# A gated linear attention followed by a maxout FFN, one core: a reversed scan makes the keys, weights are rounded and first loaded by halves, and the first packing goes out on two queues

## The chip, the cores and the metric

The kernel runs on one core of a Trainium2 chip. The metric is the device time of one execution in microseconds (us); lower is better. The engines are TensorE (PE in the profile; PEld is its weight load), VectorE (DVE), ScalarE (ACT), GpSimd (POOL) and SyncE (SP), which here only issues DMAs. ScalarE issues some too. Each engine works through its own instructions in order.

## The reference

Four batches of eight heads, 768 tokens, 48 features a head. Every head carries a 48x48 state that is decayed by a gate per feature and read by the query. The result, heads side by side, goes through an FFN that takes the maximum of three products.

```python
f = 1.0 / (1.0 + np.exp(-f_logit))
for t in range(S):
    state = f[:, :, t, :, None] * state + np.einsum('bhd,bhe->bhde', k[:, :, t], v[:, :, t])
    y[:, :, t] = np.einsum('bhd,bhde->bhe', q[:, :, t], state)
x = y.transpose(0, 2, 1, 3).reshape(B * S, H * D)           # 3072 x 384
h = np.maximum(np.maximum(x @ w1, x @ w2), x @ w3)          # 384 -> 768
out = h @ w_out                                             # 768 -> 384
```

q, k, v and f_logit come as float32, the four weight matrices as float64.

## The kernel before

**Units.** The tokens are cut into chunks of C = 64. A unit `u` is one chunk of two batches (128 tokens, all eight heads); there are NU = 24, and units 0, 2, 4, ... belong to one pair of batches, 1, 3, 5, ... to the other. Four units make a group (512 tokens), for which one FFN runs: six groups, six FFNs.

**One unit.** Gates, keys and queries are turned so that features lie on partitions: by TensorE through PSUM (`transposed`, with a ScalarE copy out) for units below 8, by VectorE's 32x32 transpose (`turned`) from unit 8 on. `sigmoids` makes the gates. `products` scans the gates forward on VectorE (L264), so that `prod` at token t is the product of the gates of its chunk up to t, held above 2^-80; a zero gate in front of each head's 64 columns together with a 1 in `floor` restarts the scan there. The query becomes `qh` = q * prod (GpSimd, L277). `quotients` takes the reciprocal of `prod` (VectorE, L283, one call per batch of the unit) and GpSimd makes `kh` = k / prod (L284). `keys` transposes `kh` back on TensorE (L297) for the state update and copies it out as `ks` (ScalarE, L299). `pairs` multiplies `kh` with `qh` (L310) and masks the scores (VectorE, L313). `values` multiplies scores with v (L327) and `ks` with v (L336) into one PSUM tile `y`; VectorE adds the old state and multiplies by the chunk's whole product (L343, L344). `finish` adds the old state's part to `y` (L357) and ScalarE evicts it into `xT`, the FFN's input, with the first three head pairs directly (L366) and the last pair through a tile `last` (L363). Six small DMAs, three per half of the partitions, pack `last` into the 16 rows that each 48 leave free in 64 (L371).

**Weights.** The float64 weights are loaded raw, as pairs of 32-bit words (L196), into four `raw` buffers, and rounded to float32 on the chip: `round_begin` makes upper bits (VectorE, L209), the rest from the low word (ScalarE, L212), adds them (GpSimd, L213) and squares the value's high word to find those too small to keep (ScalarE, L215); `round_end` merges in sign and exponent (VectorE, L223) and writes the weight or zero (VectorE, L226). A buffer is loaded anew after its `round_end`. There are 15 pieces: six of 128 columns of the three input matrices, six of 256 columns, three of 256 rows of `w_out`.

**The FFN.** `ffn` is a generator. It has 18 steps (six column blocks j, three matrices i): three kt matmuls each, 512 tokens wide (L382; the trace counts each as two), then a ScalarE copy for i = 0 (L386) or a VectorE maximum (L388). Behind them come four output steps with `w_out` (L399). In the first FFN each of the steps also rounds pieces that are needed later.

**The order** is written out by hand: units 0 to 3 first, without any FFN; then, from unit 4 on, each unit's parts with `fill(n)` between them, which takes n steps of the FFN of the group before. PSUM holds two `p` tiles for the FFN, two `tr` tiles for transposes and one tile each for scores and `y`. DMAs are issued in the order of the code on the queue named: nearly all on SyncE; before, the packing of units 0 to 2 goes to ScalarE's queue, that of unit 3 half to each. All DMAs share eight semaphores in turn, so each issue waits until the DMA that last used its semaphore has landed, on whichever queue that one was.

A second program, `general`, would run if a chunk's whole product (`ends`) fell below 2^-64; it does not with these inputs.

## Time and profile before

| | us |
|---|---|
| median of 3 runs | 551.06 (550.12 to 552.51) |
| the profiled execution | 553.05 |
| its span, first to last instruction | 551.3 |
| busy: TensorE, its weight loads | 475.6, 256.5 |
| busy: VectorE, ScalarE, GpSimd | 263.7, 127.2, 102.2 |
| first FFN matmul | 72.07 |
| first matmul of the second FFN | 187.26 |

A row of the profile's timeline gives start, duration, engine, line of the kernel, operation, tile written <- tiles read, their shape and, in brackets, how long the engine had idled before and what released it. SPq and ACTq are the DMA issues of SyncE and ScalarE. A row of groups gives the count, busy time in all, the mean of one in ns, and the idle time before them with its releasers. A row of waits gives the total, the number of times and the longest. The granted TensorE clock was 0.924 of full on average.

### The profile page before, as it was taken

The numbers are of one execution on the slowest core, as the hardware profiler recorded it, in microseconds if no ns is written. First come the engines' busy times: TensorE is split into PE (matmuls) and PEld (weight loads), VectorE is DVE, ScalarE is ACT, GpSimd is POOL, SyncE is SP. The second block draws the span as 40 slices with busy tenths as digits, with TensorE's granted clock in tenths as the row PEclk, the third lists the DMA queues.
The fourth block names the chain that finished last, engine by engine and source line by source line (L and its number), as shares of the span: only waits on it lengthen the run. The fifth ranks groups of instructions, "written<-read, shape, count | busy, mean of one in ns | idle before, by whom it ended". The sixth has DMA issues, their size and how long they took to land.

```text
span 551.3 us, 10105 instructions
## 1 busy us (share of the span) xinstructions
PE 475.6 (86%) x4067; PEld 256.5 (47%) x4067; DVE 263.7 (48%) x321; ACT 127.2 (23%) x297; POOL 102.2 (19%) x139
## 2 busy tenths in 40 slices
PE   3654067757979999999999999999999999999994
PEld 2544033333635554556445565454564445544452
DVE  5665017849457546562467545555643762011210
ACT  3253033332522122023202221222032111210000
POOL 3440014445242101220122012121201220000000
PEclk9766577959789999999999999999999999999998
DMA  9454979521251450622613515406236000100002
GB/s 135 89 139 89 175 135 168 119 61 59 37 71 44 59 86 13 78 44 50 99 33 45 77 36 74 77 9 87 42 55 97 18 4 5 47 15 0 0 15 50
DMA packets 166761, 34.99 MB, mean 63 GB/s; under 512 B 155952, under 2 KB 163632, under 8 KB 166704
## 3 DMA queue, kind: packets, MB, share of 16 engines
q1 hardware_dynamic: 163920, 33.68, 35.6%
q10 hardware_dynamic: 2784, 0.57, 0.6%
q8 instruction: 34, 0.56, 0.4%
q14 instruction: 23, 0.19, 0.1%
HBM read 28.31 MB, written 4.72 MB: 60 GB/s over the span
## 4 chain that ended last, share of the span: by engine, by line
PE 76%; DVE 6%; SPq 4%; DMA 3%; issue 3%; ACT 2%; POOL 2%; ACTq 2%; DVEq 0%; POOLq 0%
PE p L382 48%; PE p L399 17%; DVE inv L283 2%; PE y L357 2%; SPq L145 2%; PE y L327 2%; PE a L310 2%; PE tr L297 2%; SPq L196 2%; ACTq L371 2%; PE y L336 1%; DMA raw<-in_moe_w_dram 1%; POOL top_bits L213 1%; PE tr L237 1%; DMA xT<-last 1%
## 5 line engine op out<-in xcount | busy, mean ns | idle before, releaser
L382 PE MATMUL p<-xT,w_in 128*128 128x512 f32 x648 | 296.0, 609 | 23.7 <-DMA xT<-last 21.0
L382 PEld LDWEIGHTS p<-xT,w_in 128*128 128x128 f32 x648 | 122.4, 194 | 167.0 <-issue 157.6
L399 PE MATMUL p<-w_out,hm 128*128 128x384 f32 x288 | 95.3, 488 | 0.0
L283 DVE RECIPROCAL inv<-prod 128x256 f32<-128x256 f32 x48 | 82.0, 1730 | 0.3
L399 PEld LDWEIGHTS p<-w_out,hm 128*128 128x128 f32 x288 | 54.2, 190 | 38.0 <-issue 2.4
L388 DVE TENSOR_TENSOR top<-p,top 128x512 f32<-128x512 f32 x36 | 24.8, 688 | 91.1 <-PE p L382 91.1
L386 ACT COPY top<-p 128x512 f32<-128x512 f32 x36 | 21.1, 585 | 191.9 <-PE p L382 191.9
L277 POOL TENSOR_TENSOR qh<-qt,prod 128x512 f32<-128x512 f32 x24 | 28.6, 1193 | 195.2 <-DVE qt L241 176.1
L284 POOL TENSOR_TENSOR kh<-kt,inv 128x256 f32<-128x256 f32 x48 | 36.1, 753 | 77.0 <-DVE inv L283 77.0
L264 DVE TENSOR_TENSOR_SCAN prod<-gate,floor 128x520 f32<-128x520 f32 x24 | 29.7, 1238 | 29.2 <-ACT gate L253 24.0
L388 DVE TENSOR_TENSOR hm<-p,top 128x512 f32<-128x512 f32 x36 | 24.4, 678 | 39.6 <-PE p L382 39.6
L313 DVE TENSOR_TENSOR at<-a,mask 128x512 f32<-128x512 f32 x24 | 16.5, 687 | 52.8 <-PE a L310 52.8
L213 POOL TENSOR_TENSOR top_bits<-top_bits,rest_bits 128x768 uint32<-128x768 uint32 (+1 forms) x15 | 23.8, 1588 | 76.2 <-ACT rest_bits L212 38.5
L402 ACT COPY o<-p 128x384 f32<-128x384 f32 x24 | 11.5, 478 | 112.5 <-PE p L399 94.5
L297 PE MATMUL tr<-ident,kh 128*128 128x128 f32 x88 | 16.4, 318 | 22.3 <-POOL kh L284 22.2
L299 ACT COPY ks<-tr 128x512 f32<-128x512 f32 x22 | 12.9, 585 | 65.7 <-PE tr L297 62.0
L297 PEld LDWEIGHTS tr<-ident,kh 128*128 128x128 f32 x88 | 12.0, 161 | 32.9 <-POOL kh L284 26.4
L327 PEld LDWEIGHTS y<-at,v_ld 64*64 64x64 f32 x768 | 14.7, 145 | 23.2 <-issue 13.1
L327 PE MATMUL y<-at,v_ld 64*64 64x64 f32 x768 | 18.2, 237 | 8.0 <-ACT xT L366 8.0
L366 ACT COPY xT<-y 64x192 f32<-64x192 f32 (+1 forms) x72 | 22.6, 314 | 1.3
L343 DVE TENSOR_TENSOR st<-y,st 128x384 f32<-128x384 f32 x20 | 11.1, 553 | 23.9 <-PE y L336 23.9
L363 ACT COPY last<-y 64x64 f32<-64x64 f32 (+1 forms) x72 | 15.0, 208 | 21.1 <-PE y L357 16.8
(56 smaller groups left out, 278.9 us busy)
## 6 DMA issues: line engine op xcount, KB each, us to landing
v_ld<-in_v_dram SPq DMA_DIRECT2D x48, 96.0 KB, 3.0
out_dram<-o SPq DMA_DIRECT2D x48, 96.0 KB, 2.2
raw<-in_moe_w_dram SPq DMA_DIRECT2D x12, 288.0 KB, 4.3
raw<-in_moe_w_out_dram SPq DMA_DIRECT2D x3, 768.0 KB, 4.3
f_ld<-in_f_logit_dram SPq DMA_DIRECT2D x32, 64.0 KB, 2.5
k_ld<-in_k_dram SPq DMA_DIRECT2D x32, 64.0 KB, 2.5
q_ld<-in_q_dram SPq DMA_DIRECT2D x32, 64.0 KB, 2.5
xT<-last SPq DMA_DIRECT2D x123, 8.0 KB, 1.8
```

The lines of the kernel that those rows point to most:

```text
L213: nc.gpsimd.tensor_tensor(top, top, rest, op=ALU.add)
L264: nc.vector.tensor_tensor_scan(scan.rearrange("p x t -> p (x t)"), gate.rearrange("p x t -> p (x t)"), floor.rearrange("p x t -> p (x t)") ...
L277: nc.gpsimd.tensor_tensor(qh, qt, prod, op=ALU.mult)
L283: nc.vector.reciprocal(d["inv"][:, a], d["prod"][:, a])
L284: nc.gpsimd.tensor_tensor(d["kh"][:, :, a, :], d["kt"][:, a], d["inv"][:, a], op=ALU.mult)
L297: nc.tensor.transpose(tr_s[:, hp, :], kh[:, hp].rearrange("p a t -> p (a t)"), ident)
L327: nc.tensor.matmul(y[o:o + DP, a, hp * C:(hp + 1) * C], lhsT=v_ld[s, 2 * hp + par, :], rhs=d["at"][s, par, hp, :], start=(hp == 0), stop=F ...
L366: nc.scalar.copy(xT[o, :, t0 + a * C:t0 + (a + 1) * C], y[i, a, 0:NK * C].rearrange("p (h t) -> p h t", h=NK))
L382: nc.tensor.matmul(p, lhsT=w_in[i][:, kt, j * 128:(j + 1) * 128], rhs=xT[:, kt, :], start=(kt == 0), stop=(kt == NK - 1))
L386: nc.scalar.copy(top, p)
L388: nc.vector.tensor_tensor(hm[:, j, :] if i == 2 else top, p, top, op=ALU.max)
L399: nc.tensor.matmul(p[:, 0:DM], lhsT=hm[:, j, i * UT:(i + 1) * UT], rhs=w_out[:, j, :], start=(j == 0), stop=(j == NJ - 1))
```

## The change

**Keys and queries.** `products` and `quotients` become `after` and `before`. `after` scans the gates backwards on VectorE (both inputs and the output read with a step of -1), which gives for each token the product of the gates from it to the chunk's end; shifted by one column that is the factor of the keys, and its first column is the chunk's whole product. GpSimd makes `kh` in one call. `before` scans forward as the old kernel did, but starts each head at the reciprocal of the whole product (a reciprocal of 8 columns instead of 2 x 256), so that query times key is what it was. The state is now multiplied by the whole product ahead of its use, by GpSimd, and VectorE only adds.

```diff
-                nc.vector.tensor_tensor_scan(scan.rearrange("p x t -> p (x t)"), gate.rearrange("p x t -> p (x t)"),
-                                             floor.rearrange("p x t -> p (x t)"), 1.0, op0=ALU.mult, op1=ALU.max)
-                nc.gpsimd.tensor_tensor(qh, qt, prod, op=ALU.mult)
-                nc.vector.reciprocal(d["inv"][:, a], d["prod"][:, a])
-                nc.gpsimd.tensor_tensor(d["kh"][:, :, a, :], d["kt"][:, a], d["inv"][:, a], op=ALU.mult)
+            def after(u):
...
+                nc.vector.tensor_tensor_scan(r[:, 0:LEN][:, ::-1], flat(gate)[:, ::-1], flat(from_one)[:, ::-1], 1.0,
+                                             op0=ALU.mult, op1=ALU.max)
+                whole = r[:, 0:LEN].rearrange("p (x t) -> p x t", t=C + 1)[:, :, 1]
+                nc.vector.reciprocal(from_inv[u % 2][:, :, 0], whole)
+                kt = features("k", u)
...
+                nc.gpsimd.tensor_tensor(kh.rearrange("p h a t -> p a h t"), by_batch(kt),
+                                        by_batch(r[:, 1:LEN + 1].rearrange("p (x t) -> p x t", t=C + 1)[:, :, 1:]),
+                                        op=ALU.mult)
+            def before(u):
...
+                nc.vector.tensor_tensor_scan(flat(prod), flat(gate_tiles[u % 2]), flat(from_inv[u % 2]), 1.0,
+                                             op0=ALU.mult, op1=ALU.max)
+                qt = features("q", u)
...
+                nc.gpsimd.tensor_tensor(qh, qt, prod[:, :, 1:], op=ALU.mult)
+                d["qh"] = by_batch(qh)
+                if u >= 2:
+                    d["state"] = work.tile([128, 2 * HP, D], FP32, name="state")
+                    nc.gpsimd.tensor_tensor(d["state"], states[u % 2],
+                                            ends[:, u, :].unsqueeze(2).to_broadcast([128, 2 * HP, D]), op=ALU.mult)
```

In the loop over units, `after(n)` stands where `products(n)` stood, and `before(n)` behind `values(n-1)`, where the first of the two `quotients` stood. On VectorE, the rows from unit 5's first scan to its last operation before the pairs were these (`r_104` and `prod` are scans, `inv` reciprocals, `hm` and `top` FFN maxima, `st` states, the rest rounding):

```order
L264 SCALAR_TENSOR_TENSOR prod<-gate_96,floor 128x520
L388 TENSOR_TENSOR hm<-p,top 128x512
L223 SCALAR_TENSOR_TENSOR top_bits<-raw,top_bits 128x768
L226 SCALAR_TENSOR_TENSOR w_in_65<-size,top_bits 128x3x256
L209 TENSOR_SCALAR top_bits<-raw 128x768
L343 TENSOR_TENSOR st_1_129<-y,st_0_128 128x384
L344 TENSOR_TENSOR st_1_129<-st_1_129,prod 128x384
L283 RECIPROCAL inv<-prod 128x256
L223 SCALAR_TENSOR_TENSOR top_bits<-raw,top_bits 128x768
L226 SCALAR_TENSOR_TENSOR w_in_63<-size,top_bits 128x3x256
L209 TENSOR_SCALAR top_bits<-raw 128x768
L283 RECIPROCAL inv<-prod 128x256
```

and are now

```order
L301 SCALAR_TENSOR_TENSOR r_104<-gate_100,from_one 128x520
L304 RECIPROCAL from_inv_97<-r_104 128x8
L424 TENSOR_TENSOR hm<-p,top 128x512
L245 SCALAR_TENSOR_TENSOR top_bits<-raw,top_bits 128x384
L248 SCALAR_TENSOR_TENSOR w_in_65<-size,top_bits 128x3x128
L233 TENSOR_SCALAR top_bits<-raw 128x384
L376 TENSOR_TENSOR st_136<-y,state 128x384
L316 SCALAR_TENSOR_TENSOR prod<-gate_100,from_inv_97 128x520
```

What `kh` needs moved from the last row to the first; what `qh` needs moved from the first row to the last.

**Weights.** There are 12 pieces now, all of 256 columns (or rows of `w_out`), in five buffers, and each is rounded in two halves of 384 columns: 24 roundings, one in each of the first FFN's steps 0 to 11 and two in each from 12 on. Of the first three pieces the first halves are loaded ahead of the start and the second halves after unit 1.

```diff
+            RAW = 5
...
+                if len(halves) == 1:
+                    c = slice(halves[0] * 128 * words, (halves[0] + 1) * 128 * words)
+                    dst, src = dst[:, :, c], src[:, c]
...
+                if h == 1 and n + RAW < len(pieces):
+                    raw.pop(n, None)
+                    load_weight(n + RAW)
+            rounds = [(3 * (j // 2) + i, j % 2) for j in range(NJ) for i in range(3)]
+            rounds += [(9 + j // 2, j % 2) for j in range(NJ)]
...
+                            for r in [3 + step] if step < 12 else [2 * step - 9, 2 * step - 8][:24 - 2 * step + 9]:
+                                if r < len(rounds):
+                                    round_end(*rounds[r])
+                                if r + 1 < len(rounds):
+                                    round_begin(*rounds[r + 1])
```

**Packing and the order of the start.** `finish` no longer issues the packing DMAs; `pack` does, from SyncE and ScalarE for units 0 to 3, from SyncE later. Units 0 and 1 are packed behind unit 1, units 2 and 3 behind unit 3, and most loads of units 4 to 7 and of further weights come behind that.

```diff
+                for u in range(GRP):
+                    keys(u)
+                    if u == 3:
+                        finish(2, xT)
+                    pairs(u)
+                    if u < 2:
+                        sigmoids(u + 2)
+                        after(u + 2)
+                    values(u)
+                    if u < 2:
+                        before(u + 2)
+                        finish(u, xT)
+                    if u == 1:
+                        for r in rounds[0:3]:
+                            round_begin(*r)
+                        pack(0, xT, both)
+                        pack(1, xT, both)
+                        for n in range(3):
+                            load_weight(n, (1,))
+                        load(GRP)
+                    if u == 3:
+                        for r in rounds[0:3]:
+                            round_end(*r)
+                        round_begin(*rounds[3])
...
+                finish(3, xT)
+                pack(2, xT, both)
+                pack(3, xT, both)
+                load_weight(3)
+                load_weight(4)
+                load_v(GRP)
```

On SyncE, ahead of the first FFN, the packing of unit 3 (`xT<-last`) stood behind weights (`raw`) and the loads of units 4 to 6, of which the last is seen here:

```order
L196 DMA raw<-in_moe_w_dram 48x3x512
L196 DMA raw<-in_moe_w_dram 16x3x512
L145 DMA f_ld_103<-in_f_logit_dram 64x8x48 x2
L145 DMA k_ld_105<-in_k_dram 64x8x48 x2
L145 DMA q_ld_107<-in_q_dram 64x8x48 x2
L145 DMA v_ld_122<-in_v_dram 64x8x48 x2
L371 DMA xT<-last 16x128 x3
```

Now only the second weight halves and unit 4's rows stand ahead of it, and the larger pieces behind:

```order
L217 DMA raw<-in_moe_w_dram 16x3x256
L158 DMA f_ld_110<-in_f_logit_dram 64x8x48 x2
L158 DMA k_ld_112<-in_k_dram 64x8x48 x2
L158 DMA q_ld_114<-in_q_dram 64x8x48 x2
L407 DMA xT<-last 16x128 x6
L217 DMA raw<-in_moe_w_dram 48x3x512
L217 DMA raw<-in_moe_w_dram 16x3x512
```

The packing (three rows of unit 2, three of unit 3) moved ahead of the loads. At the other end of the first FFN the last pieces of `w_out` stood between the packing of units 4 and 5, ahead of the block loads of units 8 and 9 (`32x16x32` and `32x16x16`, 24 DMAs in all):

```order
L196 DMA raw<-in_moe_w_out_dram 128x2x768 x2
L371 DMA xT<-last 16x128 x6
L196 DMA raw<-in_moe_w_out_dram 128x2x768
L371 DMA xT<-last 16x128 x6
L158 DMA f_ld_102<-in_f_logit_dram 32x16x32
L158 DMA f_ld_102<-in_f_logit_dram 32x16x16
```

Now the last one stands behind the 24, whose last two are the first rows here:

```order
L171 DMA q_ld_114<-in_q_dram 32x16x32
L171 DMA q_ld_114<-in_q_dram 32x16x16
L158 DMA v_ld_128<-in_v_dram 64x8x48 x2
L217 DMA raw<-in_moe_w_out_dram 128x2x768
L407 DMA xT<-last 16x128 x6
```

It moved past the block loads, since two rounding steps per FFN step free the buffers in a different order.

214 lines of the change are left out of this document (101 added, 113 removed).

## The prediction

> **What bounds the kernel now.** I read the profile in this order: the busy slices, then two stretches side by side, then the waits, then the timeline of the front. The slices (40 equal parts of the span; tenths busy, and tenths of the TensorE clock granted) show where time can be lost at all.
>
> ```profile
> PE   3654067757979999999999999999999999999994
> PEclk9766577959789999999999999999999999999998
> ```
>
> From slice 13 (about 165 us) on, TensorE is full at full clock; only the first 165 us have holes. Next, busy time by stretch (from:to, length, then TensorE, its weight loads, VectorE, ScalarE, GpSimd; clock, DMA share, GB/s): the first FFN with units 4 to 7 between its steps, and the next group of four.
>
> ```profile
> 72.07:187.26 115.19, 94.11 (x833) 52.14 (x833) 70.02 (x79) 38.55 (x75) 42.79 (x45) 0.85 0.42 83
> 187.26:261.92 74.66, 73.98 (x686) 38.97 (x685) 40.95 (x48) 16.44 (x42) 11.39 (x16) 1.00 0.37 57
> ```
>
> A settled group takes 74.66 us, and TensorE works through 73.98 of it. VectorE has 34 us free there, so nothing saved on VectorE shortens a settled group by more than 0.7 us. What lies behind 187.26 is 551.3 - 187.3 = 364.0 us, and I keep it. The first group took 40.5 us longer than a settled one, and before it lie 72 us of start. The waits (the third from a query of 72 to 187 us on the first group) say why.
>
> ```profile
> PE p L382 <- DMA xT<-last: 21.0, 1, 21.0
> SPq L145 <- DMA xT<-last: 10.3, 4, 3.9
> PE tr L297 <- POOL kh L284: 19.9, 4, 8.9
> ```
>
> TensorE stood 21.0 us for one packing DMA, SyncE's loads waited 10.3 us for packing DMAs, and four times TensorE waited for scaled keys `kh`, which GpSimd makes from VectorE's reciprocals: 19.9 of the 21.1 us that it idled in the first group (115.19 - 94.11). The timeline shows the places in the start:
>
> ```profile
> 18.39 9.16 SPq L145 DMA_DIRECT2D v_ld<-in_v_dram  x4
> ...
> 23.17 0.65 ACT L363 COPY last<-y 128x64 f32<-128x64 f32 x3 [3.34 <-DVE st L346]
> ...
> 24.50 3.96 ACTq L371 DMA_DIRECT2D xT<-last  x6
> ...
> 39.00 0.98 ACT L366 COPY xT<-y 128x192 f32<-128x192 f32 x3
> ...
> 51.92 0.98 ACT L366 COPY xT<-y 128x192 f32<-128x192 f32 x3
> ...
> 68.93 1.87 SPq L371 DMA_DIRECT2D xT<-last  x3
> ```
>
> Unit 3 was evicted (0.65 + 0.98 us of copies) by 52.90, yet half of its packing was issued at 68.93, since on SyncE it stands behind three units' loads and twelve weight DMAs. The FFN began at 72.07.
>
> **The change, part by part. (1) The start, to the first FFN matmul.** At 0.61 an issue (the row of six further down), the four v loads take 2.4 us instead of 9.16 and end at about 21; the twelve half pieces follow by about 27 and land by 30. On ScalarE, unit 0's copies waited 3.34 us for a state behind unit 2's reciprocals (1.73 each, below); these go and a second scan of 1.24 comes, so the copies end at 23.3 by my estimate (24.80 before). `ks` of unit 1 follows at once, not behind six packing issues (3.96 us). From there to unit 1's eviction lie four copies of about 0.6, the eviction of 1.6 and two groups of matmuls: some 6 us, so 29.3 instead of 39.98. Now come three halves to round and the packing of units 0 and 1, moved to here; a half costs ScalarE two copies like the first row; the others are DMAs, with their median time to landing last:
>
> ```profile
> L212 ACT ACTIVATE rest_bits<-raw 128x384 uint32<-128x384 uint32 x6 | 3.3, 555 | 7.1 <-issue 3.9 <-DMA raw<-in_moe_w_dram 3.1
> xT<-last ACTq DMA_DIRECT2D x21, 8.0 KB, 2.5
> raw<-in_moe_w_out_dram SPq DMA_DIRECT2D x3, 768.0 KB, 4.3
> ```
>
> 3 x 2 x 0.555 = 3.3 and six issues 4.0 bring `ks` of unit 2 to 36.6. From it the path runs through that copy (0.6), six groups of small matmuls at half clock (1.1 each, the next fence), a state add (0.6) and two evictions (1.6): 11.1, so unit 3 is evicted at 47.7. Packing of units 2 and 3 follows on both queues, six issues on ScalarE. The first matmul needs the fourth landed: 47.7 + 4 x 0.66 + 2.5 = **52.8 instead of 72.07, -19.3 us**. The second weight halves queue behind the packing of unit 1 and land by about 42, before their rounding at 44 to 48. Two more memsets of 128x520 lie under the wait for the first rows. Bounds: 48, if the issues on ScalarE cost half, to 60, if a SyncE stall of 9.16 - 2.4 = 6.8 comes back elsewhere.
>
> **(2) The first group.** One wait for `kh`, a step at half clock and its like at full:
>
> ```profile
> 116.22 1.11 PE L297 MATMUL tr<-ident,kh 128*128 128x128 f32 x4 [8.93 <-POOL kh L284]
> ...
> 120.06 4.24 PE L382 MATMUL p<-xT,w_in 128*128 128x512 f32 x6
> 124.13 0.60 PE L237 MATMUL tr<-ident,k_ld 128*128 128x128 f32 x4
> 124.57 0.60 PE L237 MATMUL tr<-ident,q_ld 128*128 128x128 f32 x4
> 125.00 2.74 PE L382 MATMUL p<-xT,w_in 128*128 128x512 f32 x6
> ```
>
> What makes keys and queries costs this:
>
> ```profile
> L283 DVE RECIPROCAL inv<-prod 128x256 f32<-128x256 f32 x48 | 82.0, 1730 | 0.3
> L284 POOL TENSOR_TENSOR kh<-kt,inv 128x256 f32<-128x256 f32 x48 | 36.1, 753 | 77.0 <-DVE inv L283 77.0
> L264 DVE TENSOR_TENSOR_SCAN prod<-gate,floor 128x520 f32<-128x520 f32 x24 | 29.7, 1238 | 29.2 <-ACT gate L253 24.0 <-issue 4.6
> L277 POOL TENSOR_TENSOR qh<-qt,prod 128x512 f32<-128x512 f32 x24 | 28.6, 1193 | 195.2 <-DVE qt L241 176.1 <-ACT qt L271 19.1
> ```
>
> Per unit VectorE loses two reciprocals (3.46) and a state product, and gains a scan (1.24) and a reciprocal of 8 columns. That one is not shown: 1.73 x 8/256 = 0.05 to 1.73; I take 0.15, near the low end as its size is. VectorE gains 2.1 us a unit and the product. A scan against the direction of memory is not shown: 1.24 by the row, 2.5 at half rate; I take 1.24, the same elements (2.5 would add about 2.5 to the start, two units in series). GpSimd gets the state product of 384 columns, between 0.75 and 1.19, say 0.97, and does `kh` in one piece, 1.19 to 1.51, instead of two of 0.75. What counts is the place: `kh` needs only the first scan, two FFN steps ahead of its use, so all four waits go. In return `qh` comes late: state add, scan and product, 0.6 + 1.24 + 1.19 = 3.0, against two steps and two small groups on TensorE, 2 x 2.74 + 2 x 0.6 = 6.7. Hidden, with 3.7 to spare; if that cover goes, TensorE waits at every pair.
>
> Rounding in halves, by the longest of VectorE's three operations on a piece:
>
> ```profile
> L223 DVE SCALAR_TENSOR_TENSOR top_bits<-raw,top_bits 128x384 uint32<-128x384 uint32 x6 | 3.6, 596 | 0.0
> L223 DVE SCALAR_TENSOR_TENSOR top_bits<-raw,top_bits 128x768 uint32<-128x768 uint32 x9 | 10.3, 1146 | 1.4 <-POOL top_bits L213 1.4
> ```
>
> Two halves take 1.19 for 1.15: 0.05 more, and if the other two operations pay three times that, 18 pieces' worth is 4 us. VectorE was busy 70.0 in this stage; less 4 x 2.1, plus 4, it is 66 of some 97. Not the bound; the cover is 31 us of slack.
>
> A new wait comes with SyncE's order: the last `w_out` piece now stands behind unit 8's 24 block loads. Before, it went at 125.91, ahead of them:
>
> ```profile
> 125.91 0.37 SPq L196 DMA_DIRECT2D raw<-in_moe_w_out_dram  x1
> 141.59 3.67 SPq L371 DMA_DIRECT2D xT<-last  x6
> 145.36 4.25 SPq L158 DMA_DIRECT2D f_ld<-in_f_logit_dram  x8
> ...
> 159.34 1.41 SPq L145 DMA_DIRECT2D v_ld<-in_v_dram  x2
> ```
>
> From unit 5's eviction: packing 3.7, blocks 159.3 - 145.4 = 14.0, v 1.4, its issue 0.4 and 4.3 to land (the row further up): 23.8 us. VectorE and ScalarE meet it at step 15, after some 14 us (five steps less one already under way, plus unit 6's values and transposes), and stop in order; behind them are queued unit 7's mask and `ks`, unit 6's copies and the maxima of steps 16 and 17. TensorE can still do unit 7's scores and two steps, to 21.4. After the landing ScalarE needs two halves (2.2), `ks` (0.6) and copies (1.6): 28.2. So TensorE idles about 7, restarts at half clock (1.5 a step), and its first output waits for step 17's maximum: **+10 us**, bounds 0 and 14.
>
> Sum for the group: 74.66; transposes of four units, 4 x 3 x 0.60 = 7.2; half-clock start 4.24 - 2.74 and two transposes' 0.5 each, 2.5; late piece 10; small waits 3 (1.2 shown apart from `kh`; up to 10): 97.4 instead of 115.2, **-17.8 us**.
>
> **(3) Everything later: 0.** TensorE's full slices cover it, and the two-queue packing is for units 0 to 3 only.
>
> The sum is -19.3 - 17.8 = -37.1. The profiled execution took 553.05 (span 551.3 and 1.75 around it): 515.9. The median of the runs shown, 551.06, is 2.0 below it, so I forecast **514.0**.
>
> **The rivals.** *The piece is not late* (the 24 issues need less than their 14.0): the 10 us go, 504.0. For it: the DMA engines will be nearly idle then. Against: SyncE's issues took 0.58 each by themselves.
>
> *Loads starve the first FFN.* For it, the busiest stretch of DMA, at a share of 0.98:
>
> ```profile
> 60.00:75.00 15.00, 2.93 (x4) 1.41 (x5) 0.36 (x1) 0.00 (x0) 0.00 (x0) 0.50 0.98 147
> ```
>
> Seven pieces and three units (768 KB each) and a v load behind the last packing are 8.06 MB; at 147 GB/s that is 54.8 us from 49.6, so unit 7's rows come at 104 instead of the 101 at which they are wanted, and the last piece slides by about 9: 523.0. Against it: weight pieces with longer rows than these may move faster.
>
> *VectorE and GpSimd slow each other.* A merge that takes 1.15 on average took 1.91 here, with GpSimd at work:
>
> ```profile
> 103.39 1.91 DVE L223 SCALAR_TENSOR_TENSOR top_bits<-raw,top_bits 128x768 uint32<-128x768 uint32 x1 [1.06 <-POOL top_bits L213]
> ```
>
> The change puts more two-input work on both. If 35 us of it on VectorE (42 merges and selections of 0.6, 8 scans) double in the 37% of the stage that GpSimd is busy (42.79 of 115.19), that is 13 us more, inside the slack; but each unit's mask then comes some 2.5 late, 4 x 2.5: 524.0. Against it: the mean scan stayed at 1.24. The Trainium skill's page GPSIMD Engine Reference, section Specifications, says that GpSimd shares its SBUF interfaces with VectorE and contends with VectorE instructions that have two SBUF inputs, which the added scans have. By that rule the time is this rival's, by the mean of the scans the forecast's.
>
> *The start shortens less:* 60 at its upper bound, 521.2.
>
> *Slower.* Every pair waits for `qh`, because the forward scan is stuck behind maxima on VectorE. In settled groups the chain (3.0, and a transpose of q under 1) has three steps, 8.2 us, to hide in. To give back 37.1 in 20 units it would have to last 10.1 (1.9 over); at 11.2 they lose 60: 574.0. VectorE's 34 free us a group speak against it.
>
> **How the numbers follow.** Forecast 0.50; piece on time 0.15; starved 0.13; contention 0.10; start 0.07; late `qh` 0.05, of which 0.02 within 0.5% and 0.03 slower (0.5% is about what a measurement of this kernel can tell from no change). So faster 0.95. The range, 502 to 530, takes in the first five cases with the bounds of the small terms; late `qh`, and two bad cases at once, stay out.
>
> **What would show it.** Right: the first FFN matmul near 53, no long wait of the key transposes for `kh`, one TensorE gap of about 7 us before unit 7's values while VectorE waits for `raw`, and 364 us from the second FFN on. Wrong: gaps at earlier steps with rounding that waits for DMA (starved), long merges and late masks (contention), or pairs that wait for `qh` in settled groups.

## The result, and the profile after

| | before | after |
|---|---|---|
| median, us | 551.40 (550.12 to 552.51, 4 runs) | 531.28 (530.40 to 531.88, 4 runs) |
| profiled execution; its span | 553.05; 551.3 | 530.40; 528.3 |
| first FFN matmul | 72.07 | 55.48 |
| first group (FFN 0 with units 4 to 7) | 115.19 | 112.28 |
| from the second FFN to the end | 364.0 | 360.5 |

The ratio is 0.9635 (95% interval 0.9607 to 0.9662): 20 us faster, where 37 were forecast, and 1.3 us beyond the range. The start gave what was expected of it to within 2.7 us. The first group did not: it gained 2.9 us instead of 17.8.

The slices of the changed kernel (TensorE busy, and its granted clock):

```profile
PE   4733749987599999999999999999999999999994
PEclk9865688989889999999999999999999999999999
```

The last hole is now slice 11 (132 to 145 us); it was slice 12 (152 to 165). The same two stretches as in the prediction, the first group and a settled one (length; busy TensorE, its weight loads, VectorE, ScalarE, GpSimd; clock, DMA share, GB/s):

```profile
55.48:167.76 112.28, 91.65 (x833) 51.06 (x833) 68.11 (x102) 40.72 (x93) 49.69 (x54) 0.88 0.65 109
167.76:242.40 74.64, 74.64 (x692) 39.54 (x687) 32.15 (x46) 16.48 (x42) 13.39 (x16) 1.00 0.38 57
```

TensorE still idles 112.28 - 91.65 = 20.6 us in the first group (21.1 before), but for other things. Its waits in this stretch (waiting line and what ended the wait: total, times, longest), with the wait for the start on top:

```profile
PE p L418 <- DMA xT<-last: 10.3, 1, 10.3
PE tr L263 <- DMA f_ld<-in_f_logit_dram: 7.0, 1, 7.0
PE y L359 <- issue: 5.6, 1, 5.6
PE a L345 <- POOL qh L320: 4.7, 2, 2.4
PE y L387 <- DVE st L376: 2.2, 1, 2.2
PE y L359 <- ACT rest_bits L236: 1.1, 1, 1.1
```

No wait for `kh` is left. In its place stand unit 5's rows (7.0), unit 7's values (5.6; the list names no releaser, but the mask that they read ends at 146.40, 0.1 us before they start), the pairs and the state sum that belong to the chain of the forward scan (4.7 and 2.2), and unit 5's values (1.1). The timeline of the changed kernel shows the first of them, and what became of the start:

```profile
42.24 5.63 SPq L158 DMA_DIRECT2D f_ld<-in_f_logit_dram  x2
...
46.24 0.65 ACT L397 COPY xT<-y 64x192 f32<-64x192 f32 x2
...
50.75 4.17 SPq L407 DMA_DIRECT2D xT<-last  x6
...
55.48 5.46 PE L418 MATMUL p<-xT,w_in 128*128 128x512 f32 x6 [10.30 <-DMA xT<-last]
...
61.41 6.67 SPq L217 DMA_DIRECT2D raw<-in_moe_w_dram  x8
...
69.56 1.28 SPq L158 DMA_DIRECT2D f_ld<-in_f_logit_dram  x2
...
78.37 1.09 PE L263 MATMUL tr<-ident,f_ld 128*128 128x128 f32 x4 [6.98 <-DMA f_ld<-in_f_logit_dram]
...
79.25 4.11 PE L418 MATMUL p<-xT,w_in 128*128 128x512 f32 x6
```

Unit 3's last copies end at 46.89 (forecast 47.7), but SyncE was held by two loads of unit 4's f rows from 42.24 to 47.87, 4.3 us of it waiting for a packing DMA by its list of waits, and begins its half of the packing at 50.75. Unit 5's f rows are asked for at 69.56, behind weight pieces, and wanted at 71.39 (78.37 - 6.98); they come 7 us later, and the FFN step behind them runs at the slow rate, 4.11 us for 2.74.

### The profile page after: what moved, and what is told of

The parts are those of the page before. It is cut to its first block, busy times and chain, and to the rows that moved or that the text cites. A ratio compares the mean times of both kernels' runs of the same rounds, so it can differ in the third digit from the quotient of the medians.

```text
span 528.3 us, 10199 instructions
## 1 busy us (share of the span) xinstructions
PE 469.0 (89%) x4067; PEld 253.2 (48%) x4067; DVE 221.5 (42%) x330; ACT 129.6 (25%) x315; POOL 117.9 (22%) x148
## 4 chain that ended last, share of the span: by engine, by line
PE 75%; DMA 5%; DVE 3%; POOL 3%; issue 2%; ACT 1%; SPq 1%; ACTq 0%; DVEq 0%; POOLq 0%
PE p L418 48%; PE p L437 18%; DMA raw<-in_moe_w_dram 3%; PE y L359 2%; PE y L387 2%; PE y L368 2%; PE a L345 2%; DMA f_ld<-in_f_logit_dram 2%; POOL top_bits L237 1%; PE tr L332 1%; DVE prod L316 1%; DVE top_bits L245 1%; DMA xT<-last 1%; PE tr L263 1%; DVE w_in L248 1%
## 5 line engine op out<-in xcount | busy, mean ns | idle before, releaser
L437 PEld LDWEIGHTS p<-w_out,hm 128*128 128x128 f32 x288 | 54.7, 192 | 38.5 <-issue 3.2
L422 ACT COPY top<-p 128x512 f32<-128x512 f32 x36 | 21.1, 586 | 174.5 <-PE p L418 174.5
L307 POOL COPY ends<-r 128x8 f32<-128x8 f32 x24 | 5.6, 233 | 174.2 <-DVE r L301 174.2
L237 POOL TENSOR_TENSOR top_bits<-top_bits,rest_bits 128x384 uint32<-128x384 uint32 x24 | 27.1, 1131 | 62.7 <-DVE top_bits L233 49.6
L348 DVE TENSOR_TENSOR at<-a,mask 128x512 f32<-128x512 f32 x24 | 16.5, 688 | 52.8 <-PE a L345 52.8
L301 DVE TENSOR_TENSOR_SCAN r<-gate,from_one 128x520 f32<-128x520 f32 x24 | 30.2, 1257 | 19.2 <-ACT gate L280 14.7
L316 DVE TENSOR_TENSOR_SCAN prod<-gate,from_inv 128x520 f32<-128x520 f32 x24 | 34.8, 1449 | 0.1
L308 POOL TENSOR_TENSOR kh<-kt,r 128x512 f32<-128x512 f32 x24 | 29.5, 1228 | 13.8 <-DVE kt L267 13.8
L245 DVE SCALAR_TENSOR_TENSOR top_bits<-raw,top_bits 128x384 uint32<-128x384 uint32 x24 | 15.7, 656 | 17.2 <-POOL top_bits L237 17.1
L376 DVE TENSOR_TENSOR st<-y,state 128x384 f32<-128x384 f32 x20 | 11.0, 551 | 27.0 <-PE y L368 27.0
L334 ACT COPY ks<-tr 128x512 f32<-128x512 f32 x22 | 12.9, 586 | 38.4 <-PE tr L332 35.5
L345 PE MATMUL a<-qh,kh 48*64 48x64 f32 x768 | 16.7, 227 | 6.1 <-POOL qh L320 6.1
```

Of the source, the lines that this page charges most:

```text
L237: nc.gpsimd.tensor_tensor(top, top, rest, op=ALU.add)
L301: nc.vector.tensor_tensor_scan(r[:, 0:LEN][:, ::-1], flat(gate)[:, ::-1], flat(from_one)[:, ::-1], 1.0, op0=ALU.mult, op1=ALU.max)
L308: nc.gpsimd.tensor_tensor(kh.rearrange("p h a t -> p a h t"), by_batch(kt), by_batch(r[:, 1:LEN + 1].rearrange("p (x t) -> p x t", t=C + 1 ...
L316: nc.vector.tensor_tensor_scan(flat(prod), flat(gate_tiles[u % 2]), flat(from_inv[u % 2]), 1.0, op0=ALU.mult, op1=ALU.max)
L345: nc.tensor.matmul(p[t, par, hp * C:(hp + 1) * C], lhsT=kh[r, hp, a, :], rhs=qh[r, a, hp, :], start=True, stop=True)
L422: nc.scalar.copy(top, p)
```

## The experiments

The theories, by the letters that the expectations use. **A**: the two parts of the change add. **S**: the order of requests on SyncE's queue sets the lost time. **B**: the transfers are full, so a request moved ahead puts another behind. **C**: VectorE and GpSimd hold each other up. **D**: VectorE's queue of roundings, chained to GpSimd, stands ahead of unit 7's mask. **L**: the first group has its own end, and an earlier start only moves its waits. **H**: the hand-over between VectorE and GpSimd, apart from contention.

All times at a glance; the stages are those of each kernel's profiled run (which can lie some us off the median: e11's took 533.89), the ratio is to the kernel before on the same chip.

| kernel | median, us | ratio, 95% interval | first FFN matmul | first group | rest |
|---|---|---|---|---|---|
| the change | 531.28 | 0.9635 (0.9607 to 0.9662) | 55.5 | 112.3 | 360.5 |
| e1, last piece first | 531.76 | 0.9633 (0.9609 to 0.9657) | 55.3 | 114.9 | 360.5 |
| e2, unit 5's rows first | 524.47 | 0.9513 (0.9491 to 0.9535) | 55.0 | 106.3 | 360.7 |
| e3, unit 4's rows early | 529.05 | 0.9592 (0.9565 to 0.9619) | 55.0 | 111.0 | 360.6 |
| e4, scans alone | 526.93 | 0.9561 (0.9536 to 0.9587) | 71.5 | 92.8 | 360.5 |
| e5, fills later | 527.49 | 0.9564 (0.9540 to 0.9588) | 55.3 | 108.7 | 360.6 |
| e6, fills and piece | 527.16 | 0.9551 (0.9526 to 0.9577) | 55.6 | 109.0 | 360.6 |
| e7, start alone | 543.68 | 0.9851 (0.9807 to 0.9894) | 53.9 | 122.5 | 364.3 |
| e8, four moves | 520.36 | 0.9433 (0.9411 to 0.9455) | 54.8 | 102.1 | 360.6 |
| e9, e8 without the low bits | 507.43 | 0.9202 (0.9154 to 0.9250) | 54.9 | 88.7 | 360.6 |
| e10, e8 with qh on VectorE | 517.15 | 0.9375 (0.9336 to 0.9414) | 53.2 | 100.2 | 360.5 |
| e11, one queue | 530.85 | 0.9608 (0.9575 to 0.9640) | 56.0 | 115.3 | 360.7 |
| e12, e8, two ahead | 516.13 | 0.9354 (0.9328 to 0.9380) | 54.7 | 99.2 | 360.7 |
| e13, e10, two ahead | 514.13 | 0.9317 (0.9292 to 0.9342) | 53.8 | 97.8 | 360.6 |
| e14, the change, two ahead | 527.68 | 0.9564 (0.9538 to 0.9589) | 55.3 | 110.8 | 360.3 |

### e1: the last piece of w_out ahead of unit 8's blocks

```diff
-                    if u + 2 < NU and (u % 2 == 0 or u + 2 < BY_ROWS):
+                    if u + 2 < NU and (u % 2 == 0 and u != 6 or u + 2 < BY_ROWS):
                         load(u + 2)
 ...
                     fill(1)
+                    if u == 6:
+                        load(u + 2)
```

> The last piece of w_out is asked for ahead of unit 8's 24 block loads instead of behind them. In the changed kernel TensorE stood 5.63 us ahead of unit 7's values while ScalarE waited 7.1 us for that piece, and the step after it ran at half clock. Theory S (the order of the requests on SyncE sets the lost time): that gap goes, 5.6 us and about 1.5 us of half clock, so 523 to 526 us, and unit 8's blocks, which are wanted only 15 us later, cost nothing. Rival B (the transfers are full, a request moved ahead only puts another behind): the wait turns up at unit 8's sigmoid or transposes, within 1.5 us of the changed kernel's 531. Rival C (VectorE and GpSimd hold each other up, and the long chain behind the forward scan sets the pace): the pairs wait instead, 529 to 532 us.

Nothing: 531.8, and the wait ahead of unit 7's values is still 5.1 us. The timeline of the changed kernel had suggested the piece, since ScalarE waits for it:

```profile
134.39 1.20 POOL L146 MEMSET f_ld<- 32x512 f32 x2
...
136.72 0.55 ACT L236 ACTIVATE rest_bits<-raw 128x384 uint32<-128x384 uint32 x1 [7.08 <-DMA raw<-in_moe_w_out_dram]
136.79 1.09 POOL L146 MEMSET q_ld<- 32x512 f32 x2
...
137.96 0.99 POOL L237 TENSOR_TENSOR top_bits<-top_bits,rest_bits 128x384 uint32<-128x384 uint32 x1
...
145.71 0.69 DVE L348 TENSOR_TENSOR at<-a,mask 128x512 f32<-128x512 f32 x1
...
146.50 1.13 PE L359 MATMUL y<-at,v_ld 64*64 64x64 f32 x32 [5.63 <-issue]
```

And the same place in e1's timeline, where the piece is there and ScalarE waits for GpSimd instead:

```profile
138.70 1.09 POOL L146 MEMSET q_ld<- 32x512 f32 x2
...
139.88 0.99 POOL L237 TENSOR_TENSOR top_bits<-top_bits,rest_bits 128x384 uint32<-128x384 uint32 x1
...
140.90 0.56 ACT L236 ACTIVATE rest_bits<-raw 128x384 uint32<-128x384 uint32 x1 [7.16 <-POOL top_bits L237]
...
148.43 1.13 PE L359 MATMUL y<-at,v_ld 64*64 64x64 f32 x32 [5.10 <-issue]
```

In both, an addition (L237) follows at once on three pairs of GpSimd fills (L146). Behind that addition VectorE has three roundings, one every 2.66 us in the changed kernel, and stands 1.17 us for the addition in each of the later two; only then comes the mask (L348). The piece was late, but not last.

### e2 and e3: the rows of units 5 and 4 asked for earlier

```diff
 e2
                 load_v(GRP)
+                load(GRP + 1)
+                load_v(GRP + 1)
                 pending.append(ffn(0, xT))
 ...
                 before(GRP)
-                load(GRP + 1)
-                load_v(GRP + 1)
 e3
                     if u == 1:
+                        load(GRP)
                         for r in rounds[0:3]:
                             round_begin(*r)
 ...
                             load_weight(n, (1,))
-                        load(GRP)
```

> Unit 5's eight row loads are asked for ahead of the first FFN step, and so ahead of weight pieces 5 and 6, and not behind them. In the changed kernel TensorE waited 6.98 us for unit 5's f rows and ran the next step at half clock. Theory S: that wait goes with the slow step behind it, about 8 us, so 522 to 525 us; pieces 5 and 6 land later by the 2 to 3 us that the rows take and are still in time for roundings two or three steps later. Rival B: the rounding of piece 5 or 6 waits in place of the rows, FFN steps 9 to 12 wait for their weights, less than 3 us gained: 528 to 532 us. Rival C: the wait is hidden behind the chain of the scans, less than 3 us too, but with longer waits of the pairs for qh rather than of the FFN steps.

> Unit 4's rows are asked for ahead of unit 1's roundings and packing and not behind them, so that SyncE does not stand with its second f load (5.63 us to issue in the changed kernel) ahead of the packing of units 2 and 3. Theory S: the first FFN matmul comes at 51 to 53 us instead of 55.5, and 527 to 529 us in all. Rival B: the rows then take the transfers from the second halves of pieces 0 to 2 and from the packing, the first FFN matmul stays at 55 to 57 us, and the time within 1.5 us of 531. Rival C says nothing of the start and would have the time at 531, whatever the start does, only if the first group ends where it ended (167.8 us).

e2 gains 6.8 us; of unit 5's wait this is left, by e2's waits:

```profile
PE tr L263 <- DMA f_ld<-in_f_logit_dram: 0.2, 1, 0.2
```

Asking sooner was the cure there (S), although the transfers were full in the changed kernel (a DMA share of 1.11 and 170 GB/s between 60 and 75 us), of things not yet wanted. The landing is slow all the same: 6.0 to 8.0 us for these rows in the changed kernel, 5.8 to 7.5 in e2, against a median of 3.2 for such loads of f in before. So the wait was a late request and a slow landing together, and e2 removed the first. e3 gains 2.2 us, 0.4 of it in the start, where 2.5 to 4.5 were expected: the first FFN matmul stays at 55.0. Its timeline shows that SyncE's stall only moved: the twelve second weight halves now take it 10.13 us, up to 50.4 (8.57 in the changed kernel), and its packing begins at 50.63 instead of 50.75.

### e4: the scans alone

The kernel before, its order, loads, whole pieces and packing kept. One place of the edit:

```diff
-                products(GRP)
+                after(GRP)
                 fill(1)
-                quotients(GRP, 0)
+                before(GRP)
+                decayed(GRP)
                 fill(1)
-                quotients(GRP, 1)
```

> The kernel before with the two scans, the product of the state on GpSimd and the keys without the full reciprocal alone: its order of units, its loads, its roundings of whole pieces and its packing are those of before. If the keys' chain is what the four waits for kh came from (19.9 us in the first group of before), these go and the first group shortens by 15 to 20 us, while the first FFN matmul stays at 70 to 73 us: 531 to 537 us in all. If the roundings of whole pieces hold the chain as long as the reciprocal did, the waits only move to qh and the time is 543 to 550 us. Under Rival C the scans in the first group last over 1.6 us on average, and the time is at the upper end or above.

526.9 us: **the scans alone are 24.9 us faster than before, and 4.4 us faster than the whole change**; the two intervals in the table do not touch. The first FFN matmul is where it was (71.5), and the first group takes 92.8 us, less than was expected of it. Its waits in the group:

```profile
PE a L339 <- POOL qh L304: 3.8, 1, 3.8
PE p L407 <- DVE hm L413: 1.5, 1, 1.5
PE y L381 <- DVE st L370: 1.1, 1, 1.1
```

The forward scans in this group average 1.74 us (the reversed ones 1.24), where Rival C gave 1.6 for a time at the upper end of the range or above:

```profile
L300 DVE TENSOR_TENSOR_SCAN prod<-gate,from_inv 128x520 f32<-128x520 f32 x5 | 8.7, 1740 | 0.0
```

The time lies below the range all the same, so here the longer scans by themselves did not cost what Rival C gave them.

### e5 and e6: the GpSimd fills later, without and with the piece

```diff
-                        if n in (5, 7):
-                            pad_blocks(n // 2 % 2)
+                        if n == 5:
+                            pad_blocks(0)
+                    if u == 7:
+                        pad_blocks(1)
                     fill(1)
```

> The six GpSimd fills of the second half of the row tiles (1.1 us apiece in pairs, 3.4 us in all) are made in unit 7's iteration and not in unit 6's, where they stand ahead of the additions of the last w_out pieces. Theory D (VectorE's queue: the roundings of w_out, two in a step, each handed to GpSimd and back, stand ahead of unit 7's mask, and the fills ahead of the first of them): with the last piece still late (ScalarE had it at 136.7, GpSimd was free at 137.9) the wait of 5.6 us ahead of unit 7's values shortens by 0.5 to 1.2 us only: 529.5 to 531 us. If the fills were the whole cause, 3.5 to 5 us less: 526 to 528 us. If neither, 531.

> Both the fills later and the last piece of w_out ahead of unit 8's blocks. Theory D: the wait of 5.1 us that was left with the piece alone in front goes to 0 to 2 us, since GpSimd's addition can start at about 136 and not at 139.9: 525.5 to 528.5 us, 3 to 5 less than the changed kernel and than either edit alone. Theory S as first put (the order on SyncE alone) fell with the run of the piece alone, and would have 531 again. Rival C (VectorE and GpSimd hold each other up): the five roundings in front of the mask still take 2.7 us each whatever is ahead of them, the wait stays at 4 us or more, 529 to 531 us.

e5 gains 3.8 us by itself, more than Theory D allowed it, and the piece adds nothing to it in e6 (527.2). The expectation had the addition wait for the piece; e5's timeline shows that it had its operands already and went 3.6 us sooner than in the changed kernel, though ScalarE still waited for the next half:

```profile
134.33 0.99 POOL L237 TENSOR_TENSOR top_bits<-top_bits,rest_bits 128x384 uint32<-128x384 uint32 x1 [0.83 <-DVE top_bits L233]
...
134.58 0.56 ACT L236 ACTIVATE rest_bits<-raw 128x384 uint32<-128x384 uint32 x1 [5.74 <-DMA raw<-in_moe_w_out_dram]
...
142.88 0.75 PE L359 MATMUL y<-at,v_ld 64*64 64x64 f32 x32 [2.45 <-issue]
```

The gap ahead of the values went from 5.6 to 2.5. Unit 5's wait is 5.5 us in this run for 7.0, but the edit does not touch it, and it comes to 8.7 and 8.8 in e14 and e11: about 3 of the 3.8 us are the fills'.

### e7: the start alone

The changed kernel with forward scan, full reciprocals and double-buffered states. One place of the edit:

```diff
-                after(GRP)
+                products(GRP)
                 fill(1)
-                before(GRP)
+                quotients(GRP, 0)
                 load(GRP + 1)
                 load_v(GRP + 1)
                 fill(1)
+                quotients(GRP, 1)
```

> The changed kernel with the keys of before: forward scan, full reciprocals and products in their two halves, double-buffered states; the halves of the weights, the order of loads and units and the two queues are those of the change. Theory L (the first group has its own end, set by what must be loaded and rounded in it, and the earlier start only moves its waits): first FFN matmul at 56 to 61 us, the first group 125 us or longer, 547 to 554 us in all, next to nothing gained over before. Rival A (the two parts add, 24 us for the scans alone and the rest for the start): the first FFN matmul at 56 to 61 and the group near 115 to 118 as in before, 535 to 541 us; then the scans must be worth less in the changed kernel than alone.

543.7 us, between the two: the start comes 18 us sooner, the group takes 122.5 and gives back 7.3. Its waits in the group:

```profile
PE tr L313 <- POOL kh L306: 25.6, 4, 11.8
```

So alone the two parts are worth 24.9 and 8.1 us, together 20.1: 12.9 less than their sum. Theory L holds in part: the group ends at 164.3 with the scans alone and at 167.8 with the start added.

### e8: the four moves together

The edits of e1, e2, e3 and e5 in one kernel.

> The four moves together: unit 4's rows earlier, unit 5's rows ahead of pieces 5 and 6, the last w_out piece ahead of unit 8's blocks, the fills later. If the waits are separate, their gains add: 6.8 for unit 5's rows, 2.2 for unit 4's, 3 to 5 for the piece with the fills: 517 to 520 us, ahead of the scans alone (526.9). If the transfers as a whole bind (Rival B), what is moved ahead waits elsewhere: 523 to 526 us, with a wait for raw or for a row load of 3 us or more still in TensorE's list.

520.4 us, 10.9 less than the change, where the moves alone summed to 6.8 + 2.2 + 3.8 = 12.8. This is faster than Rival B would allow, and than the scans alone. What is left of waits in its first group is 6.2 us of pairs for `qh` in three, 2.8 ahead of unit 7's values and 3.2 of others.

### e9 and e10: GpSimd's addition left out; qh on VectorE

```diff
 e9
-                    nc.gpsimd.tensor_tensor(top, top, rest, op=ALU.add)
 e10
-                nc.gpsimd.tensor_tensor(qh, qt, prod[:, :, 1:], op=ALU.mult)
+                nc.vector.tensor_tensor(qh, qt, prod[:, :, 1:], op=ALU.mult)
```

> The kernel of the four moves, with GpSimd's addition of the weights' low bits left out (the weights lose their last bits; ScalarE still makes them). Rival C (VectorE and GpSimd hold each other up in the first group): the forward scans there come down from 1.85 us to 1.25, the pairs' waits for qh (6.2 us in three) to under 3, the wait ahead of unit 7's values (2.8) goes: 512 to 516 us, first group 102 to about 95. If only unit 7's mask is behind the roundings and the scans are slow for another reason: 517 to 519 us, the qh waits stay at 5 or more. If the loads bind what is left: within 1.5 us of 520.4.

> The kernel of the four moves, with the product qh made on VectorE straight behind the forward scan, in place of GpSimd (which took 1.17 us and began 0.1 us behind the scan). Rival C: what the pairs wait for is the scan's own length and the hand-over; on VectorE the product takes about 0.6 us, no GpSimd work lies beside it, and each of the three waits shortens by 0.5 to 1 us: 517 to 519 us. If VectorE's queue is what is full (69 of the first group's 102 us), the 0.6 us of each unit come back in the masks and the merges behind it: 520 to 522 us. From the second FFN on nothing changes (360.6 us).

Without the additions the first group takes 88.7 us, 13.4 less than e8's, and the time falls below the 512 to 516 us of Rival C. VectorE's groups in the first group of the changed kernel (merge, selection, forward scan: count, busy, mean ns, idle before them and what ended it):

```profile
L245 DVE SCALAR_TENSOR_TENSOR top_bits<-raw,top_bits 128x384 uint32<-128x384 uint32 x20 | 13.5, 676 | 15.9 <-POOL top_bits L237 15.9
L248 DVE SCALAR_TENSOR_TENSOR w_in<-size,top_bits 128x384 f32<-128x384 f32 x14 | 11.9, 848 | 1.4
L316 DVE TENSOR_TENSOR_SCAN prod<-gate,from_inv 128x520 f32<-128x520 f32 x5 | 8.2, 1639 | 0.0
```

The merges of e8, then the merges and the forward scans of e9:

```profile
L245 DVE SCALAR_TENSOR_TENSOR top_bits<-raw,top_bits 128x384 uint32<-128x384 uint32 x20 | 13.6, 681 | 13.2 <-POOL top_bits L237 13.2
...
L244 DVE SCALAR_TENSOR_TENSOR top_bits<-raw,top_bits 128x384 uint32<-128x384 uint32 x20 | 14.6, 728 | 0.2
...
L315 DVE TENSOR_TENSOR_SCAN prod<-gate,from_inv 128x520 f32<-128x520 f32 x5 | 6.4, 1276 | 0.0
```

In the changed kernel, VectorE stands 15.9 us in the group for GpSimd's additions, in order, with masks, scans and maxima behind it; e8 has 13.2 and e9 0.2. The forward scans come down from 1.65 us in e8 to 1.28, as Rival C said. Three things go at once here: the hand-over, the contention, and half of GpSimd's own work (49.6 us busy in e8's group, 25.9 in e9's). The next runs part the first two in some measure. For comparison, the merges of e4, in whole pieces with the new scans, and those of e7, in halves with the old ones:

```profile
L234 DVE SCALAR_TENSOR_TENSOR top_bits<-raw,top_bits 128x768 uint32<-128x768 uint32 (+1 forms) x11 | 11.1, 1008 | 4.6 <-POOL top_bits L224 4.6
...
L240 DVE SCALAR_TENSOR_TENSOR top_bits<-raw,top_bits 128x384 uint32<-128x384 uint32 x20 | 14.9, 743 | 12.2 <-POOL top_bits L232 12.2
```

Eleven hand-overs and 4.6 us in the one, twenty and 12.2 us in the other: the waits came with the halves and the new start, not with the scans. (The halves alone were not undone in the changed kernel.) e10 is 3.2 us under e8 and in the range expected, but not by the expected road: the product takes 1.03 us on VectorE and not 0.6, and the pairs' three waits fall only from 6.2 to 5.4 us. By the profiled runs 1.6 us lie in the start and 1.9 in the group; the intervals overlap, so the size is uncertain.

### e11: the first packing on one queue

```diff
-                both = (nc.sync, nc.scalar)
+                both = (nc.sync, nc.sync)
```

> The changed kernel with the packing of units 0 to 3 issued from SyncE alone, so 12 DMAs of a unit behind one another at 0.6 to 0.7 us each. If the two queues are worth their issue time: the first FFN matmul comes 4 us later (six more DMAs of unit 3 at 0.7 us), at 59 to 60 us, and the whole at 531 to 535 us, since the first group can take most of it up (Theory L: it ends where its own loads let it). Rival: ScalarE's issues (6 DMAs, 4.0 us, ahead of its copies) cost as much as they save, the first FFN matmul at 54 to 57 us and the time within 1.5 us of 531.3. Under Theory L the first group shortens by what the start loses; if the start counts in full, 535 us.

530.9 us, no measurable difference from 531.3. The first FFN matmul comes 0.6 us later, not 4: it did not wait for all of the twelve issues, the last of which ends 1.1 us after it began, at 57.1.

### e12, e13 and e14: the roundings begun two halves ahead

```diff
-                                if r + 1 < len(rounds):
-                                    round_begin(*rounds[r + 1])
+                                for b in [r + 1] if r < 9 else [r + 1, r + 2] if r == 9 else [r + 2]:
+                                    if b < len(rounds):
+                                        round_begin(*rounds[b])
```

> The kernel of the four moves, with each half's rounding begun two halves ahead of its end from the seventh FFN step on, and not one. Theory H (the hand-over: with one half in flight VectorE, whose queue is in order, stands until GpSimd's addition is through): VectorE's wait for the additions falls from 13.2 us to 5 or less, the group from 102.1 to 92 to 97 us, 511 to 516 us in all. Rival C (contention): GpSimd adds as much beside VectorE as before, scans stay at 1.65 us and the group at 100 to 102 us, 518.5 to 521 us.

> The same with qh made on VectorE. Theory H: both gains stand, 3 us for qh and 4 to 9 for the hand-over, 508 to 514 us. If either only filled the time that the other leaves (VectorE's queue is then full of its own work): 513 to 517 us, next to nothing over qh alone (517.2).

> The changed kernel, with nothing but the roundings begun two ahead. Theory H: the hand-overs (15.9 us of VectorE's time in the group) are on the path only where a mask, a scan or a weight is behind them; ahead of unit 7's values (5.6 us, but its fills and its late piece hold the first addition whatever is begun) and in the pairs' waits (4.7 us): 4 to 8 us less, 523 to 527 us. Rival C: 530 to 532 us. If the waits for unit 5's rows and the late piece take up what the roundings give: 528 to 530 us.

Each gains: e12 4.2 us over e8, e14 3.6 over the change, and e13 3.0 over e10 (there the intervals overlap a little). The times lie 0.1, 0.7 and 0.1 us above Theory H's ranges, and those of e12 and e14 over 2 us below Rival C's. H's other marks are missed by more: e12's group takes 99.2 us and not 92 to 97. And e13 also lies in the range that a full VectorE queue would give. e12's groups of VectorE, over 54 to 155 us:

```profile
L245 DVE SCALAR_TENSOR_TENSOR top_bits<-raw,top_bits 128x384 uint32<-128x384 uint32 x21 | 16.6, 789 | 6.3 <-POOL top_bits L237 6.3
L316 DVE TENSOR_TENSOR_SCAN prod<-gate,from_inv 128x520 f32<-128x520 f32 x6 | 9.5, 1580 | 0.0
L248 DVE SCALAR_TENSOR_TENSOR w_out<-size,top_bits 128x384 f32<-128x384 f32 x6 | 6.2, 1036 | 0.6
```

The waits for the additions fall from 13.2 to 6.3 (5 or less was expected), but the merges lengthen from 681 to 789 ns and the selections of `w_out` from 632 to 1036, and the forward scans of the group stay at 1.65 (one of the six above lies behind it): VectorE stands less for GpSimd's additions, and its own instructions beside them last longer. So H and C both have a part. What it bought is in TensorE's list: ahead of the values e8 waits 2.8 and 1.1 us and e12 0.2, while the pairs wait 7.0 us for `qh` instead of 6.2. Beginning two ahead is worth about 4 us here. The other 8.7 us between e12 and e9 are what is left of hand-overs and contention together; they were not parted further. e13, at 514.1 us, is the fastest of the kernels that compute everything: 0.9317 of before, against 0.9635 for the change.

## Why the prediction was wrong

**The start (term 1): right, mis-sized by 2.7 us.** -16.6 instead of -19.3. Every step up to unit 3's eviction held (46.9 for 47.7). What failed was taken as a bound and not as the value: "if a SyncE stall of 9.16 - 2.4 = 6.8 comes back elsewhere". It did, in unit 4's f rows, 5.63 us for two issues, ahead of the packing.

**The group without kh waits (term 2): the mechanism right.** The four waits of 19.9 us are gone, and e4 shows that alone: 92.8 us. The reversed scan costs what the forward one does, 1.24 us in the group; the reciprocal of 8 columns 0.21 for 0.15.

**The late piece (10 us of term 2): wrong.** It was late, ScalarE waited 7.1 us for it, and TensorE had the gap where the text put it, 5.6 us. But the gap is not the piece's: without the lateness it stays (e1), and it shortens with the fills alone (e5). The step that failed is the one in which VectorE and ScalarE "meet it at step 15" and "stop in order" until it lands. The fills on GpSimd, and behind them three roundings that VectorE has ahead of unit 7's mask, were on the path, and the text had neither.

**The small waits (3 us of term 2): the largest miss.** They came to 15.0 us: 7.0 for unit 5's rows, 4.7 for `qh`, 2.2 and 1.1. SyncE's queue was followed for the last piece and not for unit 5's rows, which the same change puts behind two weight pieces; e2 shows 6.8 us. `qh` was taken as hidden "with 3.7 to spare", by a chain of 3.0 us that begins as soon as `values` is through. In the changed kernel it begins late. For unit 7:

```profile
121.16 0.63 PE L368 MATMUL y<-v_ld,ks 64*64 64x48 f32 x32
...
129.59 0.55 DVE L376 TENSOR_TENSOR st<-y,state 128x384 f32<-128x384 f32 x1
...
133.28 1.13 PE L345 MATMUL a<-qh,kh 48*64 48x64 f32 x32 [2.43 <-POOL qh L320]
```

The sum that the state add reads is there at 121.79, and VectorE comes to the add 7.8 us later, behind roundings, a scan and a maximum in its queue. The chain itself then takes 3.6 us, 0.6 more than in the text, since its scan lasts 1.86.

**TensorE's own work (the 2.5 us of slow steps in term 2): mis-sized by some 6 us.** The sum has 74.66 + 7.2 + 2.5 = 84.4 us of work, 85.9 with the slow step inside the late piece; TensorE was busy 91.65 us, at a granted clock of 0.88. Slow work follows the long waits: behind unit 5's rows a step took 4.11 us for 2.74. The same work took 83.7 us at a clock of 0.98 in e9, with 5.0 us idle in the group, and 86.4 at 0.94 in e4, with 6.3 idle. So in these kernels waits and slow work came together, and a wait cost more than its own length; no run changed the one without the other.

**VectorE at "66 of some 97. Not the bound; the cover is 31 us of slack": the step that failed most.** Its busy time was right (68.1). But of the time not busy it stood 15.9 us for GpSimd, where before the merges' row showed 1.4. That is not slack: whatever stands behind in its queue is late by it. In halves there are nearly twice as many hand-overs as in whole pieces (20 for 11). e12 and e14 gain 4.2 and 3.6 us by making them overlap.

**The rest (term 3): 3.5 us better than forecast.** In before, the FFN's matmuls waited four times for ScalarE's copies from the second FFN on,

```profile
PE p L382 <- ACT top L386: 2.7, 4, 0.7
```

and none of these is left, in e4 as in the change; e7, with the full reciprocals, has the same 2.7 and 364.3 in all. The text's own bound, 0.7 us a settled group, had room for this; the sum put it at nothing.

**The rivals.** *Starved loads* came in kind: rows late behind weights, but unit 5's and not unit 7's, and asking sooner cured it (e2). *VectorE and GpSimd slow each other* came too: the forward scans went from 1.24 to 1.64 us (the reversed ones stay at 1.24) and the selections take 0.85 on average. Against this rival the text set the mean of the scans in before; in the new order the forward scans do lie beside GpSimd's work. The rule of the Trainium skill that the text weighed there (GPSIMD Engine Reference, Specifications) agrees with the trace after the change. At 523 and 524 each rival alone is 7 to 8 us short. Both came, which the range left out, and neither has the slow steps. *Late qh in settled groups* did not come: from 167.8 us on, TensorE's list has no wait.

**And the sum.** Against the forecast of 97.4 us the first group has 9.1 us more idle time (20.6, where 3 + 8.5 were allowed) and 5.8 more work. The terms were added as if the first group's length did not depend on the earlier start and what brought it. e4 and e7 show that it does: with the scans in place, the halves, the new order and a start 16 us earlier make it 19.5 us longer, 92.8 to 112.3; the three were not parted from each other. Some of that is the order of loads and the fills (e8: 102.1), some the rounding through GpSimd (e12, e9). The halves and the order that brought the earlier start cost, on balance, 4.4 us beside the scans.

## What to carry to other kernels

An engine's idle time is cover only where nothing is queued behind what it waits for: count the hand-overs as well as the busy time, and when work is cut into smaller pieces, begin them further ahead. When a stage starts earlier, list everything that it will now want earlier, and look for each in the queue that brings it. A wait that ends with a late transfer does not show that the transfer was the last thing missing; move it, and see.

## What the runs showed of the hardware

On instructions that read two tiles of SBUF, VectorE and GpSimd did not share, they took turns. From the timeline of e8 in the first group, two such instructions that overlap, three times:

```profile
82.53 1.01 POOL L237 TENSOR_TENSOR top_bits<-top_bits,rest_bits 128x384 uint32<-128x384 uint32 x1 [1.03 <-DVE top_bits L233]
...
82.77 1.86 DVE L316 TENSOR_TENSOR_SCAN prod<-gate,from_inv 128x520 f32<-128x520 f32 x1
...
96.23 1.23 DVE L301 TENSOR_TENSOR_SCAN r<-gate,from_one 128x520 f32<-128x520 f32 x1
...
96.46 1.79 POOL L237 TENSOR_TENSOR top_bits<-top_bits,rest_bits 128x384 uint32<-128x384 uint32 x1 [1.86 <-DVE top_bits L233]
...
103.15 1.17 POOL L320 TENSOR_TENSOR qh<-qt,prod 128x512 f32<-128x512 f32 x1 [1.25 <-DVE prod L316]
...
103.52 1.23 DVE L245 SCALAR_TENSOR_TENSOR top_bits<-raw,top_bits 128x384 uint32<-128x384 uint32 x1
```

In each pair the one that began first took its usual time, and the other was longer by 0.6 to 0.8 us (a merge by itself takes 0.56). A scan that begins first takes 1.23 us and GpSimd's addition 1.79 instead of 1.0; begun second, the scan takes 1.86. Of the five forward scans in this group the four that began behind a GpSimd instruction took 1.46 to 1.86 us, and the one that began ahead 1.23. VectorE's maxima and masks, which read one of their tiles from PSUM, stay at 0.64 to 0.69 us beside the same GpSimd instructions. In the three pairs the second one ends 0.4 to 1.1 us after the first, 0.1 to 0.2 us sooner than if it had started only then. The Trainium skill's page SBUF — State Buffer, section SBUF: two separate sides, says that the pair of ports is locked by whichever of the two starts first, for the whole instruction, and that the other blocks; the trace agrees with it to within these 0.2 us. So in these runs it depends on an order of a fraction of a microsecond which of the two engines pays, and the mean of a row before the change did not tell it.
